# Where splits, sums, loads and searches stand in the queues of a fused attention and Fourier kernel

## The chip, the core and the metric

The kernel runs on one core of a Trainium2 chip. The engines of the core work through their own queues, each in its given order: TensorE (PE, with its weight loads shown as PEld) multiplies matrices into PSUM, VectorE (DVE) and ScalarE (ACT) do elementwise work, GpSimd (POOL) does masks and some DMAs, and SyncE (SP) issues most DMAs. An instruction waits at the head of its queue until what it needs is there, and everything behind it on that engine waits too. The metric is the device time of one execution in microseconds, as the median of several runs.

## The reference

Two independent branches share the launch; their results stand side by side in the output.

```python
def _A_ref(x, wqkv, wo):              # x (1, 2048, 1024), 32 heads of 32
    qkv = (x @ wqkv).reshape(B, S, 3, H, Dh)...
    scores = jnp.einsum("bhqd,bhkd->bhqk", q, k) * (Dh ** -0.5)
    mask = (idx[:, None] - idx[None, :] >= 0) & (idx[:, None] - idx[None, :] < 256)
    p = _softmax(jnp.where(mask, scores, -1e9), axis=-1)
    o = jnp.einsum("bhqk,bhkd->bhqd", p, v)
    return o.transpose(...).reshape(B, S, D) @ wo

def _B_ref(x, dft_seq_re, dft_seq_im, dft_hid_re, dft_hid_im):
    a = jnp.einsum("bsd,ed->bse", x, dft_hid_re)
    b = jnp.einsum("bsd,ed->bse", x, dft_hid_im)
    return jnp.einsum("ts,bse->bte", dft_seq_re, a) - jnp.einsum("ts,bse->bte", dft_seq_im, b)
```

All inputs and the output are float32. The kernel holds each float32 operand as a pair of float16 numbers, a high and a low half, and multiplies high by high, high by low and low by high.

## The kernel before

**Splitting.** `split` (line 110) makes the pair: ACT writes the high half (scaled copy, line 112), then DVE writes the low half (the scaled value minus the high half, through `vec`, line 107). Before an operand can be split its scale must be known: the largest magnitude is searched (`top` on DVE, or `u_top` on ACT with a junk output and an accumulator), PE transposes it (`pt_...`, line 145), and DVE makes the scale from it in four small instructions (`scale_of`).

**Stages.** First come 96 products for q, k and v (24 matmuls each, `product`, line 339; the list `order`). Evictions are lines 725 to 736, and the results go to scratch in DRAM. From product 24 on, the attention runs as a generator between them: every `tick` of PE work lets it go a step on (scores `s`, line 212; exponentials; a DMA transpose of the weights `hl` to `t` on SP, line 238; masks `z` and `t` on POOL, lines 250 and 252; products `pv`, line 280), until it is used up near the end.

Then comes the Fourier branch: 64 units in four rounds (two parts p by two halves c). A round has eight x units, each with two products of 24 matmuls (hidden transform, banks `p`, `un` as weights, the matrix in `reg2`; evicted on ACT, line 913), and then eight c units (sequence transform, function `seven`, line 805). A c unit does a 2 by 2 block product with seven products of 12 matmuls instead of eight, at positions 0 to 6; positions 0 to 3 and 6 are evicted by ACT (lines 809 and 824), positions 4 and 5 are added to what is there by DVE (line 811), and position 6 uses the bank of position 4 again. After position 5 and position 6 a finished 128 by 1024 result goes out, in round 0 by a plain DMA on SP, later as an accumulating store by POOL (line 952). The sums that the seven products need are made on DVE (`u_step`, line 626: raw pieces are split as `un_a`, `reg`, `un_c`, `un_b`, with four additions and subtractions, line 624, between).

Last come eight units `po` of the same seven products for the attention's output matrix wo. Its pieces are loaded, subtracted and split during the last three c units (`wo_blocks`, line 760), and the attention's output is summed in `o_blocks` (line 781, sums `r` at line 788).

**What sets the order.** The text of the kernel gives a list of things to do after each product: `do(n, turn, f, ...)` puts `f` behind position `turn` of unit n. A scheduler then lays the instructions of every engine in a queue by a timeline of its own, and may draw instructions forward or back as long as data and buffers allow. `tc.issue_after(ins)` adds an edge: what is traced in its block comes behind `ins` in the queue of their engine. `behind_act[0]` is the latest eviction that was traced on ACT, `behind[0]` the latest addition on DVE. All raw pieces of 128 by 1024 float32 (512 KB) go through a ring of six buffers, `rawp`; a load waits for the last reader of the piece six before it. The matrix of part p = 1 comes as eight pieces `wd1_...`, loaded and split into `reg2` during round 1's c units.

## Time and profile before

| | us |
|---|---|
| median of 3 runs | 1848.59 |
| runs | 1844.81 to 1850.34 |
| profiled execution, own time | 1843.89 |
| its span | 1842.1 |
| busy: PE, DVE, ACT, POOL | 1762.1, 1323.3, 1091.9, 415.7 |
| mean granted TensorE clock | 0.985 of full |

The page of the profile gives busy times, a picture of the span in 40 slices, the chain that ended last and the costliest groups. A line of the timeline reads: start in us, duration, engine, line of the kernel, instruction, what it writes and reads, sizes, count; in brackets the idle time of the engine before it and the instruction whose end released it. Buffer numbers are left out there: `p_a`, `p_b`, `p_c` are the three banks of a c unit, `raw_u` any raw piece of a unit.

In time, the q, k and v products end at about 576 us; the rounds' x units begin at about 576, 839, 1130 and 1401 us, and the `po` units at 1686.

### The profile page before, as it was taken

How to read it: one execution, taken by the hardware profiler on the slowest of the kernel's cores; microseconds unless marked ns; L12 is line 12 of the kernel's file. 1: busy time of each engine (PE TensorE's matmuls, PEld its weight loads, DVE VectorE, ACT ScalarE, POOL GpSimd, SP SyncE). 2: the span in 40 equal slices, each digit the busy share in tenths (PEclk: the TensorE clock that was granted, in tenths of full speed). 3: DMA queues.
4: the chain of work that ended last, by engine and by line, in shares of the span. 5: the costliest groups of instructions: out<-in, count | busy, mean ns of one | idle time of the engine just before them, and what ended most of it. 6: DMA issues, size and time to landing. Idle time of an engine off the chain costs nothing.

```text
span 1842.1 us, 30059 instructions
## 1 busy us (share of the span) xinstructions
PE 1762.1 (96%) x10876; PEld 857.9 (47%) x10876; DVE 1323.3 (72%) x2362; ACT 1091.9 (59%) x1867; POOL 415.7 (23%) x666
## 2 busy tenths in 40 slices
PE   7999999999999999999989899999989999888998
PEld 3444545445555545544544444545444544333443
DVE  7665787787666798776788786798776788486441
ACT  3333455465555687766777776787666787453222
POOL 0000222122213332322233234223333323100000
PEclk9999999999999999999999999999999999999999
DMA  5357899887757547778458899558999548754431
GB/s 228 122 181 204 218 236 231 220 230 171 171 127 184 117 119 182 186 180 195 101 129 187 187 200 210 104 120 185 155 163 208 118 92 140 193 108 85 122 92 69
DMA packets 440596, 297.95 MB, mean 162 GB/s; under 512 B 339072, under 2 KB 396416, under 8 KB 440448
## 3 DMA queue, kind: packets, MB, share of 16 engines
q1 hardware_dynamic: 433536, 270.87, 61.1%
q0 software_dynamic: 6912, 25.17, 8.4%
q8 instruction: 85, 1.39, 0.3%
q14 instruction: 63, 0.52, 0.1%
HBM read 146.93 MB, written 75.63 MB: 121 GB/s over the span
## 4 chain that ended last, share of the span: by engine, by line
PE 68%; DVE 10%; DMA 7%; issue 7%; ACT 6%; POOL 2%; SPq 0%; DVEq 0%; ACTq 0%; POOLq 0%
PE p L345 12%; PE p_a L817 11%; PE pk L345 9%; PE pq L345 8%; PE pv L345 8%; PE p_b L817 5%; PE po_a L817 5%; PE pv L280 3%; PE s L212 3%; DMA t<-hl 2%; PE p_c L817 2%; PE po_b L817 2%; DMA raw_wd<-in_wd_dram 2%; PE po_c L817 1%; DMA ot<-ohl 1%
## 5 line engine op out<-in xcount | busy, mean ns | idle before, releaser
L345 PE MATMUL p<-reg,un 128*128 128x512 f16 x1536 | 349.2, 379 | 5.6 <-ACT un L112 3.3
L232 ACT ACTIVATE s<-s,bias,escs 128x256 f32<-128x256 f32 (+1 forms) x512 | 269.5, 528 | 10.5
L225 ACT ACTIVATE bias<-mx,pshift,escs 128x2 f32<-128x2 f32 x256 | 98.2, 384 | 245.0 <-DVE mx L222 221.0
L236 DVE TENSOR_TENSOR hl<-s,hl 128x512 f16<-128x512 f32 (+1 forms) x256 | 170.3, 666 | 87.7 <-ACT hl L235 83.8
L345 PEld LDWEIGHTS <-un 128*128 128x128 f16 x1536 | 146.2, 98 | 169.5 <-ACT un L112 3.8
L229 POOL TENSOR_SCALAR mark<-bias 128x1 f32<-128x1 f32 x128 | 45.2, 353 | 770.7 <-ACT bias L225 770.7
L817 PE MATMUL p_a<-reg,un_c 128*128 128x512 f16 x768 | 182.6, 383 | 9.3 <-ACT y L809 5.8
L345 PE MATMUL pq<-reg,wu_q 128*128 128x512 f16 x768 | 177.5, 385 | 7.0 <-ACT reg L112 4.3
L345 PE MATMUL pk<-reg,wu_k 128*128 128x512 f16 x768 | 174.4, 379 | 0.7 <-ACT wu_k L112 0.4
L252 POOL TENSOR_SCALAR_AFFINE_SELECT t<-t 128x512 f16<-128x512 f16 x224 | 174.9, 807 | 0.1
L345 PE MATMUL pv<-reg,reg 128*128 128x512 f16 x768 | 173.6, 379 | 0.0
L222 DVE TENSOR_REDUCE mx<-s 128x2 f32<-128x512 f32 (+1 forms) x256 | 170.1, 666 | 2.5
L250 POOL TENSOR_SCALAR_AFFINE_SELECT z<-t 128x512 f16<-128x512 f16 x224 | 159.9, 735 | 51.6 <-DMA t<-hl 44.5
L235 ACT ACTIVATE hl<-s 128x512 f16<-128x512 f32 (+1 forms) x256 | 148.6, 581 | 8.7 <-DMA t<-hl 3.9
L220 DVE COPY_PREDICATED s<-upper,s 128x256 f32<-128x256 uint32 x224 | 94.3, 422 | 70.1 <-PE s L212 66.2
L212 PE MATMUL s<-qk,qk 96*128 96x128 f16 (+2 forms) x704 | 129.1, 274 | 2.3 <-DVE hl L236 1.6
L817 PEld LDWEIGHTS <-un_b 128*128 128x128 f16 x768 | 74.3, 99 | 96.6 <-issue 17.8
L345 PEld LDWEIGHTS <-wu_q 128*128 128x128 f16 x768 | 74.6, 99 | 95.5 <-issue 12.1
L280 PE MATMUL pv<-vt,t 128*128 128x65 f16 x1984 | 111.2, 186 | 8.2 <-POOL t L252 8.1
L817 PEld LDWEIGHTS <-un_c 128*128 128x128 f16 x768 | 74.5, 98 | 94.5 <-issue 11.3
L817 PEld LDWEIGHTS <-un_a 128*128 128x128 f16 x768 | 74.6, 100 | 88.7 <-issue 10.3
L345 PEld LDWEIGHTS <-reg 128*128 128x128 f16 x768 | 73.6, 98 | 83.2
(175 smaller groups left out, 2895.4 us busy)
## 6 DMA issues: line engine op xcount, KB each, us to landing
raw_u<-in_cs_dram SPq DMA_DIRECT2D x64, 512.0 KB, 4.6
qk<-qs SPq DMA_DIRECT2D x192, 128.0 KB, 3.5
out_dram<-y POOLq DMA_DIRECT2D x36, 512.0 KB, 8.0
raw_u<-in_xb_dram SPq DMA_DIRECT2D x32, 512.0 KB, 4.5
vs<-yv SPq DMA_DIRECT2D x32, 260.0 KB, 2.5
vt<-vs SPq DMA_DIRECT2D x32, 260.0 KB, 3.8
raw_x<-in_xa_dram SPq DMA_DIRECT2D x16, 512.0 KB, 10.2
qs<-yq SPq DMA_DIRECT2D x32, 256.0 KB, 2.3
```

The costliest lines, as they stand in the source:

```text
L212: nc.tensor.matmul(s[:, j, at:at + (k1 - k0) * P], q2s[g, sc][:, h, i * P:i * P + P], k2s[g, k0 // QB][:, h, k0 % QB * P:k0 % QB * P + (k1 ...
L220: nc.vector.copy_predicated(s[:, :, 2 * P:3 * P], upper2, s[:, :, :P] if nb == 3 else never2)
L222: nc.vector.tensor_reduce(mx, sv, axis=AX.X, op=ALU.max, negate=True)
L225: nc.scalar.activation(bias, mx, AF.Identity, bias=pshift, scale=es)
L232: nc.scalar.activation(sv[:, h], sv[:, h], AF.Exp, bias=bias[:, h:h + 1], scale=es)
L235: nc.scalar.activation(hi, sv, AF.Copy)
L236: behind[:] = [nc.vector.tensor_tensor(lo, sv, hi, op=ALU.subtract)]
L250: nc.gpsimd.affine_select(out=z, in_=pk, compare_op=ALU.is_gt, fill=0.0, base=0, pattern=[[0, 4], [-1, P]], channel_multiplier=1)
L252: nc.gpsimd.affine_select(out=pk, in_=pk, compare_op=ALU.is_ge, fill=0.0, base=0, pattern=[[0, 4], [1, P]], channel_multiplier=-1)
L280: nc.tensor.matmul(pvt[:, r, j, lo:], weights(part, j, kb), vts[g, k // QB][:, k % QB, at + lo:at + VW], start=(m == 0), stop=(m == len(se ...
L345: nc.tensor.matmul(ps, lhs(hl, d), rhs(hr, d), start=(m == 0), stop=(m == 3 * n - 1))
L817: nc.tensor.matmul(ps, lhs[pos](hl, k), rhs(pos)[:, hr, k], start=(m == 0 and pos < 2), stop=(m == 11), skip_group_check=True)
```

## The change

Four edits:

1. `split` takes an instruction `after`; its ACT half is then issued behind it. All splits of the units and of the `wd` pieces now pass the latest eviction.
2. In `wo_blocks` the differences (`minus`) and in `o_blocks` the two sums `r` are issued behind the latest addition on DVE.
3. Loads of c-unit pieces move from positions 5 and 6 to 1 and 3 (3 and 4 in round 1); the `wd` pieces are loaded after position 1 instead of 2 and split after position 5 instead of 3.
4. The searches of a c unit's two pieces are made in the other order, and two units ahead at positions 1 and 3 instead of 2 and 5.

```diff
-    def split(hi, lo, raw, s):
-        nc.scalar.activation(hi, raw, AF.Copy, scale=s)
+    def split(hi, lo, raw, s, after=()):
+        with tc.issue_after(after[0].ins) if after else nullcontext():
+            nc.scalar.activation(hi, raw, AF.Copy, scale=s)
...
     def wd_split():
-        piece_split(*waiting.pop(0))
+        piece_split(*waiting.pop(0), behind_act)
...
-        if j == 0:
+        if j == 1:
             tops[key] = small.tile([P, 2], F32, tag="top2", name=f"top_{key}")
...
-        if j == 1:
+        if j == 0:
             spread(key, 2)
...
-            split(u[:, 0], u[:, 1], raws.pop((n, 0)), vB[:, 1:2])
+            split(u[:, 0], u[:, 1], raws.pop((n, 0)), vB[:, 1:2], behind_act)
...
-            split(t[:, 0], t[:, 1], src, s)
+            split(t[:, 0], t[:, 1], src, s, behind_act)
...
-            split(t[:, 0], t[:, 1], r2[:, 4:], s)
+            split(t[:, 0], t[:, 1], r2[:, 4:], s, behind_act)
...
-            with tc.issue_after(behind_act[0].ins):
-                split(o[:, 0, 2 * i:2 * i + 2], o[:, 1, 2 * i:2 * i + 2], raw, vwo[:, 1:2])
-        return [lambda: (fill(0, b1), sub(b2, b2, b1)), lambda: (fill(6, b4), sub(b4, b4, b2)),
-                lambda: (fill(3, b3), sub(b1, b4, b1)), lambda: (fill(4, b2), sub(b3, b3, b4)),
+            split(o[:, 0, 2 * i:2 * i + 2], o[:, 1, 2 * i:2 * i + 2], raw, vwo[:, 1:2], behind_act)
+        def minus(o, a, b):
+            with tc.issue_after(behind[0].ins):
+                sub(o, a, b)
+        return [lambda: (fill(0, b1), minus(b2, b2, b1)), lambda: (fill(6, b4), minus(b4, b4, b2)),
+                lambda: (fill(3, b3), minus(b1, b4, b1)), lambda: (fill(4, b2), minus(b3, b3, b4)),
...
-            nc.vector.tensor_tensor(r.rearrange("p a g t -> p (a g) t"), t[:, :, 0], t[:, :, 1], op=ALU.add)
+            with tc.issue_after(behind[0].ins):
+                nc.vector.tensor_tensor(r.rearrange("p a g t -> p (a g) t"), t[:, :, 0], t[:, :, 1], op=ALU.add)
...
-                    look = (n - 2, 2), (n - 2, 5), (n - 2, 6)
+                    look = (n - 2, 1), (n - 2, 3), (n - 2, 6)
...
-                do(*look[0], u_top, n, 0)
-                do(*look[1], u_top, n, 1)
+                do(*look[0], u_top, n, 1)
+                do(*look[1], u_top, n, 0)
...
-                        do(c0 + j, 2, wd_load, 1, (j + 1) // 4, (j + 1) % 4)
-                    do(c0 + j, 3, wd_split)
+                        do(c0 + j, 1, wd_load, 1, (j + 1) // 4, (j + 1) % 4)
+                    do(c0 + j, 5, wd_split)
...
+            turns = (3, 4) if r == 1 else (1, 3)
             for j in range(3, 8):
-                do(c0 + j - 3, 5, u_load, c0 + j, 1)
-                do(c0 + j - 3, 6, u_load, c0 + j, 0)
+                do(c0 + j - 3, turns[0], u_load, c0 + j, 1)
+                do(c0 + j - 3, turns[1], u_load, c0 + j, 0)
             if r < 3:
                 for j in range(4):
-                    do(c0 + 5 + j // 2, 5 + j % 2, u_load, c0 + 8 + j)
+                    do(c0 + 5 + j // 2, turns[j % 2], u_load, c0 + 8 + j)
```

No instruction is added or removed; the queues of PE, DVE, ACT, POOL and SP are laid out anew from the middle of the v products on. Three places follow. In them the rows carry the numbers of the tiles: `un61_c` is a split operand of unit 61, `p2_60_a` bank a of c unit 60, `p1_49_0` the first product of x unit 49, `raw_wo1_0` a piece of wo, `raw_wd1_1_0` the fifth piece of the matrix of part 1.

DVE after unit 61's sums, in the wo stretch, before:

```order
L624 TENSOR_TENSOR raw_u61_0_18207<-raw_u61_0_18207,raw_u61_1_18182 128x512
L624 TENSOR_TENSOR raw_wo1_0_18509<-raw_wo1_0_18509,raw_wo0_0_18507 128x1024
L107 SCALAR_TENSOR_TENSOR un61_c_18439<-raw_u61_1_18182,sc_u61_18362,un61_c_18439 128x1024
L107 TENSOR_REDUCE top1_u62_18473<-top_u62_18424 128x1
L624 TENSOR_TENSOR raw_wo1_1_18517<-raw_wo1_1_18517,raw_wo0_1_18515 128x1024
L811 SCALAR_TENSOR_TENSOR y2_6359<-p2_60_a_18373,fu60_18205,y2_6359 128x512
L811 SCALAR_TENSOR_TENSOR y2_6359<-p2_60_b_18374,fu60_18205,y2_6359 128x512
L107 TENSOR_REDUCE sc_u62_18491<-pt_u62_18492 128x1
L107 SCALAR_TENSOR_TENSOR un61_b_18455<-raw_u61_0_18207,sc_u61_18362,un61_b_18455 128x1024
```

and with the change:

```order
L625 TENSOR_TENSOR raw_u61_0_18119<-raw_u61_0_18119,raw_u61_1_18083 128x512
L107 SCALAR_TENSOR_TENSOR un61_c_18441<-raw_u61_1_18083,sc_u61_18364,un61_c_18441 128x1024
L107 TENSOR_REDUCE top1_u62_18445<-top_u62_18409 128x1
L816 SCALAR_TENSOR_TENSOR y2_6359<-p2_60_a_18373,fu60_18207,y2_6359 128x512
L816 SCALAR_TENSOR_TENSOR y2_6359<-p2_60_b_18374,fu60_18207,y2_6359 128x512
L625 TENSOR_TENSOR raw_wo1_0_18509<-raw_wo1_0_18509,raw_wo0_0_18507 128x1024
L107 TENSOR_REDUCE sc_u62_18493<-pt_u62_18494 128x1
L107 SCALAR_TENSOR_TENSOR un61_b_18462<-raw_u61_0_18119,sc_u61_18364,un61_b_18462 128x1024
```

The first wo difference has moved behind the two additions of unit 60, the second one (`raw_wo1_1`) out of the piece, some twenty rows further down.

ACT around the split of the fifth `wd` piece, in round 1's c units, before:

```order
L809 ACTIVATE reg1_81<-p2_27_c_11690,fu27_11412 128x512
L232 ACTIVATE s_159_11615<-s_159_11615,bias_159_11629,escs_111 128x256
L235 ACTIVATE hl_159_11635<-s_159_11615 128x512
L112 ACTIVATE reg2_82<-raw_wd1_1_0_11768,vwd_102 128x1024
L809 ACTIVATE y0_6357<-p2_27_a_11688,fu27_11412 128x512
L611 ACTIVATE junk_6356,top_u29_11766<-raw_u29_0_11686 128x1024
```

and with the change:

```order
L814 ACTIVATE y2_6359<-p2_28_b_11916,fu28_11686 128x512
L113 ACTIVATE reg1_81<-raw_u29_1_11562,sc_u29_11906 128x512
L612 ACTIVATE junk_6356,top_u30_12026<-raw_u30_1_11839 128x1024
L814 ACTIVATE y1_6358<-p2_28_c_11917,fu28_11686 128x512
L113 ACTIVATE reg2_82<-raw_wd1_1_0_11751,vwd_102 128x1024
L301 ACTIVATE ohl_4_3_11966<-o_4_3_11522 128x512
```

The split has moved from unit 27 to unit 28. Its load on SP stands in both orders behind the attention's transpose `t_157`, so that two blocks of attention (`hl_158` and `hl_159`) lay between before and six (to `hl_163`) lie between now.

ACT around the split of x unit 50, before (unit 47 is a c unit of the round before):

```order
L112 ACTIVATE un49_16341<-raw_u49_0_15767,sc_B_101 128x1024
L232 ACTIVATE s_225_16042<-s_225_16042,bias_225_16064,escs_111 128x256
L235 ACTIVATE hl_224_16018<-s_224_15996 128x256
L112 ACTIVATE un50_16460<-raw_u50_0_16000,sc_B_101 128x1024
L232 ACTIVATE s_225_16042<-s_225_16042,bias_225_16064,escs_111 128x256
```

and with the change:

```order
L919 ACTIVATE y1_6358<-p1_48_1_16344,tf_103 128x512
L233 ACTIVATE s_229_16283<-s_229_16283,bias_229_16305,escs_111 128x256 x2
L236 ACTIVATE hl_229_16311<-s_229_16283 128x512
L919 ACTIVATE y2_6359<-p1_49_0_16388,tf_103 128x512
L113 ACTIVATE un50_16460<-raw_u50_0_15860,sc_B_101 128x1024
L226 ACTIVATE bias_230_16375<-mx_230_16373,pshift_93,escs_111 128x2
```

Unit 50's split has moved from the end of the round before to right behind the eviction of unit 49's first product, half a unit ahead of its use.

More of the change, by code (lines that the diff above doesn't have):

```diff
@@ L423, in wv_top, with piece_split @@
         spread(f"wv{vh}", 4)
-    def piece_split(half, i, raw, s):
-        split(reg2[:, half, 0, 2 * i:2 * i + 2], reg2[:, half, 1, 2 * i:2 * i + 2], raw, s)
+    def piece_split(half, i, raw, s, after=()):
+        split(reg2[:, half, 0, 2 * i:2 * i + 2], reg2[:, half, 1, 2 * i:2 * i + 2], raw, s, after)
     def wv_finish(vh):
```

## The prediction, on record before the run

> **What bounds the kernel now.** I read the page first, then the busy time by stretch, then every idle gap of TensorE (PE) in the timeline with what ended it, and last the other engines around the largest gaps.
>
> ```profile
> PE 1762.1 (96%) x10876; PEld 857.9 (47%) x10876; DVE 1323.3 (72%) x2362; ACT 1091.9 (59%) x1867; POOL 415.7 (23%) x666
> ```
>
> PE works through 96% of the span, so nothing but PE's own gaps (about 80 us) can be won, and each new gap is paid in full. Where they lie (columns: stretch, its length, busy us of PE, PEld, DVE, ACT, POOL, granted clock, DMA share, GB/s):
>
> ```profile
> 840.00:945.00 105.00, 99.86 (x648) 49.15 (x646) 83.62 (x142) 75.70 (x134) 29.76 (x39) 0.98 0.61 136
> 945.00:1105.00 160.00, 149.31 (x978) 73.57 (x977) 128.01 (x247) 116.47 (x203) 45.32 (x70) 0.98 0.88 182
> 1105.00:1225.00 120.00, 116.47 (x798) 58.38 (x797) 91.13 (x156) 86.14 (x151) 43.42 (x59) 1.00 0.70 149
> 1225.00:1385.00 160.00, 149.03 (x979) 74.24 (x978) 123.99 (x246) 112.02 (x201) 53.41 (x74) 0.96 0.90 164
> 1385.00:1495.00 110.00, 108.50 (x731) 53.98 (x729) 81.15 (x145) 80.07 (x143) 34.31 (x50) 0.98 0.70 139
> 1606.00:1686.00 80.00, 62.13 (x269) 26.95 (x268) 62.02 (x75) 38.17 (x46) 5.93 (x7) 0.91 0.55 119
> ```
>
> The rows are, in turn, x units and c units of round 1, the same of round 2, the x units of round 3, and the last three c units, in which the wo pieces are prepared. PE is idle 5.1, 10.7, 3.5, 11.0, 1.5 and 17.9 us. The worst stretch is the last, and VectorE (DVE) is as busy there as PE.
>
> **The wo stretch (sums behind additions).** PE's gaps and the DVE rows that end them (start, duration, instruction, in brackets the idle time before it and its releaser):
>
> ```profile
> 1609.30 0.32 PE L145 MATMUL pt_u<-ident,top_u 128*128 128x128 f32 x1 [3.03 <-DVE top_u L107]
> 1614.77 4.09 PE L817 MATMUL p_a<-reg,un_b 128*128 128x512 f16 x12 [5.15 <-DVE y L811]
> 1636.01 0.32 PE L145 MATMUL pt_u<-ident,top_u 128*128 128x128 f32 x1 [1.60 <-DVE top_u L107]
> 1636.66 2.75 PE L817 MATMUL p_a<-reg,un_b 128*128 128x512 f16 x12 [0.33 <-DVE y L811]
> 1660.79 4.97 PE L817 MATMUL p_a<-reg,un_b 128*128 128x512 f16 x12 [5.84 <-DVE y L811]
> 1670.26 0.59 PE L817 MATMUL p_a<-reg,un_c 128*128 128x512 f16 x2 [1.91 <-ACT p_c L824]
> ...
> 1606.75 1.23 DVE L624 TENSOR_TENSOR raw_wo<-raw_wo,raw_wo 128x1024 f32<-128x1024 f32 x1 [9.50 <-DMA raw_wo<-in_wo_dram]
> 1612.83 1.23 DVE L624 TENSOR_TENSOR raw_wo<-raw_wo,raw_wo 128x1024 f32<-128x1024 f32 x1 [3.59 <-DMA raw_wo<-in_wo_dram]
> 1613.97 0.74 DVE L811 SCALAR_TENSOR_TENSOR y<-p_a,fu,y 128x512 f32<-128x512 f32 x1
> 1620.66 1.29 DVE L107 SCALAR_TENSOR_TENSOR un_a<-raw_u,sc_u,un_a 128x1024 f16<-128x1024 f32 x1 [1.91 <-ACT un_a L112]
> 1629.46 1.28 DVE L107 SCALAR_TENSOR_TENSOR reg<-raw_wo,sc_wo,reg 128x1024 f16<-128x1024 f32 x1 [4.61 <-ACT reg L112]
> ```
>
> Two differences of wo pieces stand in DVE's queue ahead of unit 60's additions and wait for loads (9.50 and 3.59 us); the addition starts at 1613.97, straight after the second, and PE has by then lost 3.03 + 5.15. The gap before 1660.79 is the same addition of unit 62 behind DVE work that nobody waits for yet. The listed gaps make 17.9 us, and after the two long ones twelve products take 4.09 and 4.97 instead of 2.75: 3.6 more, so 21.5 us are lost. The change puts both additions of unit 60 ahead of every wo difference, and the second round of r sums behind unit 63's additions. How short can the stretch get? PE needs 62.1 - 3.6 = 58.5. DVE has 62.0 of work, of which the two r sums, four differences and two splits of the second block (7 us at this row's kind of duration) leave the stretch: 55, and its waits of 1.91 and 4.61 stay, because the fills hang on the same evictions as before: 61.5. Something is late next: unit 61's un_b split now stands behind the first wo difference, and the load may come 3 us later because PE's last attention block does; I allow 1.5. So 80 becomes 63: **17 us gained**. If nothing stands behind anything it is 21.5; if DVE keeps its other idle time (18 us in the row) and only the 9.5-us half of the defect goes, it is 8.
>
> **The wd pieces of round 1.** Rows of SyncE's queue (SP), ScalarE (ACT) and PE:
>
> ```profile
> 1020.18 0.44 SPq L99 DMA_DIRECT2D raw_wd<-in_wd_dram  x1
> ...
> 1026.64 1.15 ACT L112 ACTIVATE reg<-raw_wd,vwd 128x1024 f16<-128x1024 f32 x1 [5.81 <-DMA raw_wd<-in_wd_dram]
> ...
> 1028.41 5.28 PE L817 MATMUL p_a<-reg,un_c 128*128 128x512 f16 x12 [4.24 <-ACT y L809]
> 1034.30 2.75 PE L817 MATMUL p_b<-reg 128*128 128x512 f16 x12
> ```
>
> The split was queued a block or two of attention after its load; ACT stood 5.81 us, the eviction behind it came late, PE waited 4.24 and then ran at half pace (5.28 against 2.75). In the new order six blocks lie between load and split where two did, so the wait goes: 4.24 + 2.53, and some 0.6 for lesser ones: **7.4 us**. From below 0, if SP still issues the load late; from above 9.
>
> The granted clock drops after such gaps (0.91 in the wo stretch). The Trainium skill, "TensorE: Matmul & The Clock Gate", Part 1, says that PE falls to half clock after an idle window of about 3.4 us and needs as much busy time to come back; an estimate from that page is 1.7 us for each of the gaps of 4.24, 5.15 and 5.84, 5.1 together where the rows give 6.1, and the sum would be 1 us smaller. The trace disagrees on the threshold too:
>
> ```profile
> 1570.02 4.28 PE L817 MATMUL p_a<-reg,un_a 128*128 128x512 f16 x12
> ```
>
> this slow dozen follows gaps of only 2.20 and 0.94 us; the rows decide.
>
> **Loads apart from the accumulating stores.** No instruction goes; 64 loads of c units are issued two to five products earlier, while POOL's stores stay at positions 5 and 6. What they may relieve:
>
> ```profile
> 1307.22 6.64 SPq L238 DMA_TRANSPOSE t<-hl  x2
> 1313.95 8.29 SPq L303 DMA_TRANSPOSE ot<-ohl  x1
> ...
> 1318.67 0.80 POOL L250 TENSOR_SCALAR_AFFINE_SELECT z<-t 128x512 f16<-128x512 f16 x1 [6.91 <-PE s L212]
> ...
> PE pv L280 <- POOL z L250: 11.3, 6, 4.3
> PE pv L280 <- POOL t L252: 8.1, 7, 1.8
> ```
>
> Behind two loads and two stores SP takes 6 to 8 us over one or two transposes, the masks on POOL come late, and PE waits 19.4 us in all for them. The bytes are the same and a load still meets the previous unit's stores (8 us to land); between 0 and 19.4 I take **4**, nearer to nothing, since most of the crowd is the transposes themselves. The Trainium skill, "DMA: Bandwidth & Descriptors", section "Issuing engines are not separate DMA queues", says that DMAs of SP and GpSimd run interleaved on the same 16 engines; read strictly, the same bytes then take the same time and this term is 0, the sum 4 us higher.
>
> **Splits behind evictions: the x units.** Before, units 1 to 6 of a round were split two units ahead; now only after the first eviction of the unit before, 24 units in all. What covers it:
>
> ```profile
> 1190.98 0.69 ACT L913 ACTIVATE y<-p,tf 128x512 f32<-128x512 f32 x1
> ...
> 1197.07 3.19 PE L345 MATMUL p<-reg,un 128*128 128x512 f16 x14
> ...
> 1459.65 0.67 ACT L913 ACTIVATE y<-p,tf 128x512 f32<-128x512 f32 x1
> ...
> 1464.16 6.85 PE L345 MATMUL p<-reg,un 128*128 128x512 f16 x31
> ...
> 1210.22 1.04 PE L345 MATMUL p<-reg,un 128*128 128x512 f16 x4 [1.30 <-ACT un L112]
> 1212.61 6.87 PE L345 MATMUL p<-reg,un 128*128 128x512 f16 x31 [1.36 <-DVE un L107]
> ...
> L112 ACT ACTIVATE un<-raw_u,sc_B 128x1024 f16<-128x1024 f32 x32 | 36.5, 1143 | 0.4 <-PE p_a L817 0.4
> L107 DVE SCALAR_TENSOR_TENSOR un<-raw_u,sc_B,un 128x1024 f16<-128x1024 f32 x32 | 41.6, 1303 | 19.5 <-ACT un L112 19.3
> ```
>
> From the end of that eviction to the next unit's first product there are 5.4 us (1191.67 to 1197.07) and, in a tight case, 3.8 (1460.32 to 1464.16). The pair takes 1.14 + 1.30 = 2.4, so DVE may be 1.4 to 3 us late before PE notices. Unit 39 (1210.22) was split this late already and cost 1.30 + 1.36, but there another split and three copies stood between eviction and split; in the new order the split mostly stands right behind. I take 2 us for the 24; the bounds are 0 and 24 x 2.66 = 64. A round's seventh unit stays late; in rounds 0 and 3 its scale's transpose has only 2 to 3 us of PE work behind it instead of about 6, which I price at unit 39's 2.66 each, less what they lose now: **4 us lost**.
>
> **Splits and searches of the c units.** The searches come one or two products earlier in the program, yet in the new order un_c stands only 6 to 13 ACT instructions ahead of the eviction that follows its product, in ten of the fourteen later c units of rounds 0 and 2, where it stood 14 to 22 ahead; before, some c units of round 1 stood like that, with
>
> ```profile
> 968.03 0.59 PE L817 MATMUL p_a<-reg,un_c 128*128 128x512 f16 x2 [0.61 <-ACT p_c L824]
> 979.38 2.75 PE L817 MATMUL p_b<-reg 128*128 128x512 f16 x12 [0.60 <-ACT y L809]
> 1015.80 0.59 PE L817 MATMUL p_a<-reg,un_c 128*128 128x512 f16 x2 [0.41 <-ACT p_c L824]
> ```
>
> gaps of 0.4 to 0.6, a little more with what follows: 0.7 x 10 units = **7 us lost**, between 0 (attention fills) and twice that. The wd pieces of the first half move from the stretch around 400 us to 430 to 540, beside products that hardly wait: nothing; uncovered they would cost ACT's 8 x 1.15 = 9 us.
>
> **The sum.** Gains 17 + 7.4 + 4 = 28.4, losses 2 + 4 + 7 = 13: 15 us less. The profiled execution took 1843.89 us (span 1842.1 and 1.8 around it) and becomes 1828.5. It stands 4.7 under the median of the runs, so the median goes from 1848.6 to **1833**.
>
> **The rivals.** *More is won* (0.12): the crowd of transposes dissolves as well. For it: 19.4 us of PE waits hang on it; against it: the same bytes. Another 12, and the c units' 7 do not come: 1814. *DVE is the bound in the wo stretch* (0.15): its 62 us of work and its own waits stay, 8 instead of 17 are won, and with the losses 6 remain: 1842. For it: the row, where DVE equals PE; against it: half of DVE's 18 us of idle time was waits on loads. *The x units stall* (0.18), the other side: DVE, in order and 76% busy in 1105 to 1225, takes the low half late, and PE waits at each unit's third product as before 1212.61. It decides once the pair ends more than 3.8 to 5.4 us after the eviction. 24 x 1.36 = 33 in place of the 2: 1848.6 - 17 + 33 = 1864. Against it: the pair's 2.4 us. That the change does nothing is out, since hundreds of rows move on PE, DVE, ACT and SP.
>
> **Chances and range.** The forecast has 0.55, with 1820 to 1843 of its own. About 0.3% (5.5 us) is what a measurement here can tell. Faster: 0.52 of the forecast, 0.12, and 0.05 of the DVE case: 0.69. Same: 0.03 and 0.08: 0.11. Slower: 0.18 and 0.02 of the DVE case: 0.20. The range 1812 to 1860 takes in the larger win and an x-unit stall of up to 1.1 us per unit.
>
> **What would show it.** Right: no PE gap over 2 us after unit 60's additions and the last stretch near 63 us; no ACT wait on raw_wd in round 1; x units with gaps under 0.5 us. Wrong: PE waits on un at most x units; un_c or un_b as releasers in every c unit of rounds 0 and 2; a new long wait of DVE on a wo load with PE behind it.

## The result, and the profile after

The changed kernel takes 1845.27 us (median of 12 runs, 1834.52 to 1849.41); the kernel before, run beside it, takes 1845.20 (12 runs). The ratio is 0.999, with a 95% interval of 0.9971 to 1.0009: no change that these runs can tell. The forecast was 15 us less. Two executions further down, of 2305.85 and 2176.07 us, ran at a granted clock of 0.75 and 0.80; the ratios leave them out, while the medians given hold them.

The page's first part, of the changed kernel:

```profile
PE 1766.4 (96%) x10876; PEld 859.8 (47%) x10876; DVE 1321.2 (72%) x2362; ACT 1087.0 (59%) x1867; POOL 397.9 (22%) x666
```

The totals are close to those of before; by place the two kernels differ. The busy time by stretch of the changed kernel (columns as in the prediction: stretch, its length, busy us of PE, PEld, DVE, ACT, POOL, granted clock, DMA share, GB/s):

```profile
663.00:703.00 40.00, 36.84 (x206) 16.95 (x206) 31.79 (x58) 28.07 (x52) 6.41 (x8) 0.87 0.51 112
...
951.00:1115.00 164.00, 148.08 (x937) 71.64 (x935) 127.92 (x242) 117.96 (x205) 46.91 (x67) 0.96 0.89 172
...
1503.00:1539.00 36.00, 30.83 (x182) 14.56 (x181) 31.01 (x56) 25.92 (x49) 9.53 (x13) 0.91 0.44 95
...
1623.07:1685.94 62.87, 58.50 (x271) 26.31 (x269) 56.42 (x68) 37.01 (x44) 5.95 (x7) 1.00 0.72 167
```

and of the kernel before, over the same products as the last of these rows (from the last products of unit 60 to the first `po` product):

```profile
1605.90:1685.80 79.90, 62.03 (x269) 26.85 (x268) 62.02 (x75) 38.16 (x45) 5.93 (x7) 0.91 0.54 118
```

So the wo stretch shrank from 79.9 to 62.9 us, at full clock: 17.0 us won. The first and the third row of the changed kernel are new losses: the passage to the first c unit of rounds 0 and 3, with PE idle 3.2 and 5.2 us and a granted clock of 0.87 and 0.91.

To compare places that lie at other times in each kernel, I took from the trace the time from each start of a PE matmul to the next, less the usual time for a matmul of that shape, and summed it from the first product of one unit to the first of another. This lost time holds idle gaps and half pace together. By unit, in us, of the kernel before, the changed kernel and, for later, the freed kernel of the experiments:

```
units        before   changed   freed
start to 6     22.7      21.3    17.8
6 to 10         4.2      12.9     7.4
10 to 15        3.3       2.1     1.7
15 to 18        0.2       4.0     0.2
18 to 24        3.6       5.3     4.3
24 to 31       20.7      24.4     5.7
31 to 40        4.9       3.8    12.6
40 to 47       17.3      11.8     8.3
47 to 54        0.5       1.7     2.9
54 to 57        5.2      12.3     8.2
57 to 60        5.5       5.9     6.0
60 to 63       20.6       2.8     2.8
63 to end       9.1       9.3     9.3
sum           117.9     117.8    87.3
```

In the changed kernel 17.8 us are won from unit 60 to 63, and 19.6 lost from 6 to 10, 15 to 18 and 54 to 57. What ended PE's waits, over the whole span (columns: us in total, times, longest):

```profile
PE pv L281 <- POOL z L251: 17.1, 8, 4.3
PE pv L281 <- POOL t L253: 6.5, 7, 1.9
...
PE p_b L822 <- DVE top_u L107: 5.2, 3, 2.9
...
PE p_b L822 <- ACT un_b L113: 3.6, 3, 2.3
...
PE pv L281 <- DMA t<-hl: 2.1, 1, 2.1
...
PE p_a L822 <- ACT un_a L113: 1.9, 1, 1.9
...
PE p L346 <- DVE un L107: 1.0, 1, 1.0
```

Waits on `un_b`, a name that the same list of before doesn't have, are new. The first c unit of round 0 shows how they arise; ACT, then DVE, then PE of the changed kernel:

```profile
673.42 0.69 ACT L919 ACTIVATE y<-p,tf 128x512 f32<-128x512 f32 x1 [6.59 <-PE p L346]
674.00 1.14 ACT L113 ACTIVATE un_c<-raw_u,sc_u 128x1024 f16<-128x1024 f32 x1
...
678.76 0.68 ACT L919 ACTIVATE y<-p,tf 128x512 f32<-128x512 f32 x1
679.33 1.14 ACT L113 ACTIVATE un_b<-raw_u,sc_u 128x1024 f16<-128x1024 f32 x1
...
682.02 1.27 DVE L107 SCALAR_TENSOR_TENSOR un_b<-raw_u,sc_u,un_b 128x1024 f16<-128x1024 f32 x1
683.21 0.14 DVE L107 TENSOR_REDUCE top_u<-top_u 128x1 f32<-128x2 f32 x1
...
680.68 0.59 PE L822 MATMUL p_b<-reg,un_b 128*128 128x512 f16 x2
683.35 3.06 PE L822 MATMUL p_b<-reg,un_b 128*128 128x512 f16 x7 [2.07 <-DVE top_u L107]
```

and the same of the kernel before:

```profile
668.43 1.15 ACT L112 ACTIVATE un_c<-raw_u,sc_u 128x1024 f16<-128x1024 f32 x1 [0.68 <-DVE raw_u L624]
669.48 1.13 ACT L112 ACTIVATE un_b<-raw_u,sc_u 128x1024 f16<-128x1024 f32 x1
670.52 0.67 ACT L913 ACTIVATE y<-p,tf 128x512 f32<-128x512 f32 x1
...
675.55 2.11 PE L817 MATMUL p_b<-reg,un_b 128*128 128x512 f16 x9
```

Before, ACT made both splits ahead of the first eviction of x unit 7, in time that it had to spare. In the changed kernel it stands idle for 6.59 us until that eviction can run, splits `un_c` behind it and `un_b` behind the second one. PE reaches `un_b` at 680.68, its low half is finished at 683.29, and PE waits 2.07 us and then runs seven matmuls in 3.06 where nine took 2.11. The row names `top_u` as the releaser because that small reduction ended last on DVE; what PE needs is the row above it, `un_b`. Unit 56 loses the same way, 2.31 and 2.85 us at 1519.06 and 1522.52.

A second loss stands ahead of this one, at unit 8's first split, `un_a`; rows of ACT and PE of the changed kernel:

```profile
661.29 1.13 ACT L113 ACTIVATE un_a<-raw_u,sc_u 128x1024 f16<-128x1024 f32 x1
...
662.48 0.60 PE L822 MATMUL p_a<-reg,un_a 128*128 128x512 f16 x2 [1.87 <-ACT un_a L113]
663.52 1.89 PE L346 MATMUL p<-reg,un 128*128 128x512 f16 x4 [0.24 <-ACT un L113]
```

PE transposes unit 8's search result at 656.65 (653.03 before), so the scale is ready at about 661 and PE waits 1.87 us for `un_a`; four matmuls after it take 1.89 us, where the kernel before has four in 1.04.

### The profile page after: what moved, and what is told of

Its sections match the earlier page's. It is cut to its first block, busy times and chain, and to the rows that moved or that the text cites. A ratio compares the mean times of both kernels' runs of the same rounds, so it can differ in the third digit from the quotient of the medians.

```text
span 1843.2 us, 30061 instructions
## 1 busy us (share of the span) xinstructions
PE 1766.4 (96%) x10876; PEld 859.8 (47%) x10876; DVE 1321.2 (72%) x2362; ACT 1087.0 (59%) x1867; POOL 397.9 (22%) x666
## 4 chain that ended last, share of the span: by engine, by line
PE 69%; issue 11%; DVE 8%; DMA 5%; POOL 4%; ACT 2%; SPq 0%; POOLq 0%; DVEq 0%; ACTq 0%
PE p_a L822 12%; PE p L346 11%; PE pv L346 9%; PE pk L346 8%; PE pq L346 7%; PE p_b L822 6%; DMA t<-hl 5%; PE po_a L822 5%; PE pv L281 3%; PE s L213 3%; PE p_c L822 3%; PE po_b L822 2%; POOL t L253 2%; POOL z L251 2%; DVE raw_u L625 1%
## 5 line engine op out<-in xcount | busy, mean ns | idle before, releaser
L230 POOL TENSOR_SCALAR mark<-bias 128x1 f32<-128x1 f32 x128 | 49.2, 384 | 843.7 <-ACT bias L226 823.8
L822 PE MATMUL p_a<-reg,un_c 128*128 128x512 f16 x768 | 187.8, 389 | 3.7 <-ACT p_c L829 3.5
L251 POOL TENSOR_SCALAR_AFFINE_SELECT z<-t 128x512 f16<-128x512 f16 x224 | 153.3, 703 | 60.2 <-DMA t<-hl 58.2
L253 POOL TENSOR_SCALAR_AFFINE_SELECT t<-t 128x512 f16<-128x512 f16 x224 | 160.5, 741 | 0.2
L281 PE MATMUL pv<-vt,z 128*128 128x65 f16 (+1 forms) x896 | 97.8, 187 | 18.8 <-POOL z L251 17.1
## 6 DMA issues: line engine op xcount, KB each, us to landing
raw_x<-in_xa_dram SPq DMA_DIRECT2D x16, 512.0 KB, 10.2
```

Source lines behind the costliest of these rows:

```text
L251: nc.gpsimd.affine_select(out=z, in_=pk, compare_op=ALU.is_gt, fill=0.0, base=0, pattern=[[0, 4], [-1, P]], channel_multiplier=1)
L253: nc.gpsimd.affine_select(out=pk, in_=pk, compare_op=ALU.is_ge, fill=0.0, base=0, pattern=[[0, 4], [1, P]], channel_multiplier=-1)
L281: nc.tensor.matmul(pvt[:, r, j, lo:], weights(part, j, kb), vts[g, k // QB][:, k % QB, at + lo:at + VW], start=(m == 0), stop=(m == len(se ...
L822: nc.tensor.matmul(ps, lhs[pos](hl, k), rhs(pos)[:, hr, k], start=(m == 0 and pos < 2), stop=(m == 11), skip_group_check=True)
```

## The experiments

All ratios are to the kernel before, run in the same sessions. Differences between two changed kernels are of their medians, which can come from different sessions; the kernel before had medians of 1843.34 to 1846.07 us in them, so 3 us of such a difference mean little. Rows are of one execution: those of the freed kernel, of the wd part alone and of the first unit's edge alone took 1813.22, 1878.09 and 1880.38 us, 7, 14 and 15 us less than the medians, and their rows explain no more than these executions lost.

**The wo part alone.** The kernel before, with the differences and r sums behind the latest addition:

```
+        def minus(o, a, b):
+            with tc.issue_after(behind[0].ins):
+                sub(o, a, b)
...
+            with tc.issue_after(behind[0].ins):
                 nc.vector.tensor_tensor(r..., t[:, :, 0], t[:, :, 1], op=ALU.add)
```

> The kernel before with one part of the change: the wo differences, the r sums and the wo splits in their new places, nothing else. Theory T (the wo stretch wins what was forecast, and splits behind evictions around the start of a round's c units give it back): 17 to 18 us less than before, about 1828, and the profile shows TensorE's lost time from unit 60 to unit 63 fall from about 20 to about 3 us. Rival D (VectorE is the bound; time won there comes back in the output units): within 4 us of before, with new gaps after unit 63. Rival C (the DMA crowd sets the total and only moves about): within 5 us of before, with mask waits larger elsewhere.

1829.09 us against 1845.57; ratio 0.9909 (0.9879 to 0.9938): 16.5 us less. Lost time from unit 60 to 63 fell from 20.6 to 6.5, and nothing came back behind unit 63 (8.6 against 9.1). Theory T holds for this part; the rivals that the gain comes back elsewhere fall.

**The splits behind evictions, with and without the first c unit.** First all of them alone on the kernel before:

```
+        with tc.issue_after(after[0].ins) if after else nullcontext():
+            nc.scalar.activation(hi, raw, AF.Copy, scale=s)
...
-            split(u[:, 0], u[:, 1], raws.pop((n, 0)), vB[:, 1:2])
+            split(u[:, 0], u[:, 1], raws.pop((n, 0)), vB[:, 1:2], behind_act)
```

> The kernel before with one part of the change: the splits of the x units and c units behind the latest eviction. Theory T: 10 to 18 us more than before (1855 to 1863), lost at the seventh x unit, the first c unit and the second c unit's start of rounds 0 and 3 and at the start of round 1; from one x unit to the next under 0.5 us. Rival C (the crowd of DMAs carries the loss, not the splits): within 5 us of before. Rival S (the prediction's stall of every x unit): 30 us more, 1.4 at each x unit.

1879.70 us, 1.0176 (1.0141 to 1.0212): 34 us more, twice what theory T allowed. Unit 6 to 10 loses 13.8 us, the x units from 18 to 22 nothing that differs from before by 1 us. Rival S falls: the x units as such do not stall.

Then the changed kernel with the first c units free ("the freed kernel"):

```
-        s = su[n]
+        s, after = su[n], behind_act if i else ()
...
-            split(t[:, 0], t[:, 1], src, s, behind_act)
+            split(t[:, 0], t[:, 1], src, s, after)
```

> The changed kernel, with the splits of the first c unit of each round (units 8, 24, 40, 56) free of the eviction edge again, as before the change; all other edges stay. Theory T: most of the loss at units 7 to 9 (9.6 us), 55 to 57 (4.6) and some at round 1 (3.8) returns: 8 to 15 us less than the changed kernel, 1830 to 1837. Rival C: within 4 us of the changed kernel. Rival X (the x units' own splits, 7 and 55 above all, carry the loss): 0 to 4 us less.

1820.18 us, 0.9852 (0.9820 to 0.9885): 25 us less than the changed kernel. ACT's splits of unit 8 in its timeline stand ahead of the eviction again, and PE does not wait:

```profile
666.38 1.15 ACT L113 ACTIVATE un_c<-raw_u,sc_u 128x1024 f16<-128x1024 f32 x1 [3.08 <-DVE raw_u L625]
667.43 1.13 ACT L113 ACTIVATE un_b<-raw_u,sc_u 128x1024 f16<-128x1024 f32 x1
668.47 0.67 ACT L919 ACTIVATE y<-p,tf 128x512 f32<-128x512 f32 x1
...
675.55 2.11 PE L822 MATMUL p_b<-reg,un_b 128*128 128x512 f16 x9
```

The win is larger than T's 8 to 15. By the table above, 13.4 of the 30.5 us of lost time between the two profiled executions lie from 6 to 10, 15 to 18 and 54 to 57; the largest piece, 18.7, lies in round 1's c units (24 to 31), of which only the first was edited. The late `un_a` stays: PE waits 1.87 us for it here too, at 658.95, and from 6 to 10 still loses 7.4 us against 4.2 before.

> The changed kernel without the eviction edge on any split of x and c units; the wd and wo splits keep theirs. Theory T: 10 to 18 us less than the changed kernel, 1827 to 1835. Rival C: within 4 us of the changed kernel. Rival X: clearly less than the kernel that frees the first c units alone.

With no eviction edge on any of these splits: 1829.69 us, 0.9921 (0.9893 to 0.9949). That is 15.6 less than the changed kernel but 9.5 more than the freed one: in this company the edges on the other splits win something.

> The changed kernel, with only the first c units of rounds 0 and 3 (units 8 and 56) free of the eviction edge; units 24 and 40 keep it. In the profiles the freed kernel and the changed one differ by 9 us from unit 7 to 9, by 19 from unit 24 to 31 and by 4 from unit 54 to 57. If each unit's edge is paid where it stands: 9 + 4 = 13 us less than the changed kernel, 1832, and round 1 stays as it is in the changed kernel (19 us dearer than in the freed one). If the loss of round 1 is the crowd of transposes, which the first delay puts into another place, round 1 comes out different although nothing was changed there: 1818 to 1826.

```
+        s, after = su[n], () if n in (8, 56) else behind_act
```

1832.27 us, 0.9925 (0.9896 to 0.9954): 13.0 less than the changed kernel, the sum that was expected if each unit's edge is paid where it stands. But it is not paid quite there. Lost time from 6 to 10 falls by 3.9 and from 54 to 57 by 8.6; 15 to 18 and 24 to 31, where nothing was edited, fall by 3.8 and 9.9, and 31 to 40 rises by 10.3. The freed kernel, in which units 24 and 40 are free as well, loses 8.8 us less still from 24 to 31. The total agrees with the sum, the places with both theories in part.

> The changed kernel, with only the third split (un_b) of the first c unit of a round free of the eviction edge. In the changed kernel it ends 2.6, 1.7, 0.5 and 3.4 us after TensorE first needs it, while un_c has 6 to 12 us to spare. Theory: un_b alone carries the direct loss, so 10 us less than the changed kernel at least, about 1825 (1818 to 1835). Rival: within 5 us of the changed kernel, since un_b still stands behind un_c, which stays behind the first eviction.

```
+            split(t[:, 0], t[:, 1], src, s, () if i == 0 and k == "b" else behind_act)
```

1829.44 us, 0.9916 (0.9885 to 0.9946): 15.8 of the 25 us hang on the edge of `un_b` alone. From 6 to 10, 15 to 18 and 54 to 57, where the freed kernel wins 13.4 us, this one wins about 12 by the same count, and PE has no wait on `un_b` at unit 8. So most of the loss at these places hangs on `un_b`.

**The three other parts, each alone on the kernel before.**

> The kernel before with one part of the change: the loads of the c units two to five products earlier. Forecast of this part: 4 us less, 1841.5, from mask waits that fall from 19.4 us. Rival (the same bytes take the same time, so the crowd only moves): within 3 us of before, mask waits still 15 to 25. Rival (earlier loads meet the spills of attention): 5 us more.

```
+            turns = (3, 4) if r == 1 else (1, 3)
...
-                do(c0 + j - 3, 5, u_load, c0 + j, 1)
-                do(c0 + j - 3, 6, u_load, c0 + j, 0)
+                do(c0 + j - 3, turns[0], u_load, c0 + j, 1)
+                do(c0 + j - 3, turns[1], u_load, c0 + j, 0)
```

1846.76 us, 0.9998 (0.9975 to 1.0020). PE's waits on masks, of this kernel:

```profile
PE pv L280 <- POOL z L250: 13.7, 7, 4.9
PE pv L280 <- POOL t L252: 7.8, 10, 2.1
```

21.5 in all, 19.4 before. The loads relieve nothing.

> The kernel before with one part of the change: the searches of the c units one or two products earlier and in the other order. Forecast of this part by itself: no more than 3 us either way, since ScalarE is busy at two thirds and only the scale's place (unchanged at position 6) decides. Rival (a search waits for a raw piece that is not there yet and holds up the evictions behind it): 5 to 10 us more, with waits of ScalarE on raw_u.

```
-                    look = (n - 2, 2), (n - 2, 5), (n - 2, 6)
+                    look = (n - 2, 1), (n - 2, 3), (n - 2, 6)
```

1845.50 us, 1.0002 (0.9982 to 1.0022). The total is the same, its parts are not: PE's waits on POOL's masks fall to 11.1 us, while ACT's waits on wd pieces, whose splits were not touched, grow from 23.2 to 30.1 and PE waits 13.6 us for the evictions behind them (5.8 before).

> The kernel before with one part of the change: loads and splits of the wd pieces in their new places. Forecast of this part: 7.4 us less, 1838, with the wait of the split on its piece (5.81 us) and the gap of 4.24 us gone. Rival (the load is late again, or the time is lost at masks in the next units): within 3 us of before.

```
-        piece_split(*waiting.pop(0))
+        piece_split(*waiting.pop(0), behind_act)
...
-                        do(c0 + j, 2, wd_load, 1, (j + 1) // 4, (j + 1) % 4)
-                    do(c0 + j, 3, wd_split)
+                        do(c0 + j, 1, wd_load, 1, (j + 1) // 4, (j + 1) % 4)
+                    do(c0 + j, 5, wd_split)
```

1892.52 us, 1.0256 (1.0219 to 1.0294): 47 us more, which no theory had. The wait itself is gone: the view of the tile `raw_wd` has, for this kernel,

```profile
its engine sat idle before it (us, times) until:
  ACT reg L113: 7.3, 8
```

and no DMA, where the kernel before has

```profile
  DMA raw_wd<-in_wd_dram: 23.2, 12
```

The time went to the masks (33.0 us of waits against 19.4) and to one wait of 10.2 us in the wo stretch, at unit 62's transpose, behind a difference that waited 15.8 us for its load:

```profile
PE pv L281 <- POOL z L251: 25.8, 10, 6.3
PE pt_u L146 <- DVE top_u L107: 12.0, 3, 10.2
...
PE pv L281 <- POOL t L253: 7.2, 9, 1.4
```

Lost time grows most from 31 to 47 (48.2 us against 22.2), where only the last wd piece, in unit 31, is left to split. The edge also moves ACT's splits of the first half of the matrix, from 362 to 393 us to 417 to 458, and PE's order differs from 367 us on; which half costs the 47 us was not separated.

> The kernel before, with the wd loads and splits at their new turns but without the eviction edge on the splits. The queues are then those of the kernel before, except that the loads stand earlier in SyncE's. If the 47 us of the whole wd part come from the edge: within 4 us of before, and ScalarE's waits on wd pieces (23.2 us before) a little less. If they come from the turns: 30 us more or worse.

The same without `behind_act`: 1844.12 us, 0.9996 (0.9978 to 1.0014). The queues of PE, DVE and ACT are then those of before, since the scheduler draws the splits forward to their old places. The turns do nothing; the edge does everything, for better (the wait on the pieces) and worse.

**Does a part have a price of its own?** The wd edge taken out of the freed and out of the changed kernel:

```
-        piece_split(*waiting.pop(0), behind_act)
+        piece_split(*waiting.pop(0))
```

> The freed kernel (first c units without the eviction edge), with the eviction edge taken off the wd splits too; their turns stay. In the queues the attention blocks 180 to 255 then have 100 products of TensorE between a block's scores and its weighted sum, where the freed kernel has 98 (180 to 219) and 88 (220 to 255). Cover theory (the wd edge costs because it makes TensorE's order leave the masks less time): 4 to 10 us less than the freed kernel in rounds 2 and 3, against up to 7 us of ScalarE's waits on wd pieces that come back in round 1: 1812 to 1822. Rival W (the edge on the wd splits is what wins round 1): 5 to 10 us more than the freed kernel, lost at units 25 to 28, 1825 to 1830.

1854.88 us, 1.0054 (1.0028 to 1.0080): 35 us more than the freed kernel. The cover theory fails, rival W has the sign and a quarter of the size. ACT's waits on the pieces are back, and PE's behind them, with masks on top; its waits on masks and evictions, and two of ACT's rows:

```profile
PE pv L281 <- POOL z L251: 21.1, 8, 6.0
PE p_a L822 <- ACT y L814: 14.1, 4, 6.5
PE pv L281 <- POOL t L253: 8.3, 7, 3.5
...
1010.13 1.15 ACT L113 ACTIVATE reg<-raw_wd,vwd 128x1024 f16<-128x1024 f32 x1 [4.96 <-DMA raw_wd<-in_wd_dram]
1038.15 1.15 ACT L113 ACTIVATE reg<-raw_wd,vwd 128x1024 f16<-128x1024 f32 x1 [4.45 <-DMA raw_wd<-in_wd_dram]
```

> The changed kernel with the eviction edge taken off the wd splits alone. Between scores and weighted sums of blocks 180 to 219 there are then 106 products where the changed kernel has 88 (before: 108), and 102 against 86 in blocks 220 to 255 (before: 99). Cover theory: 10 to 25 us less than the changed kernel, 1820 to 1835, with mask waits down from 24 us. Rival W: 5 to 10 us more than the changed kernel.

1847.25 us, 1.0011 (0.9992 to 1.0030): 2 us more than the changed kernel, which is within the noise. Neither theory. The cover came back as counted, and mask waits went to 27.4 us all the same. So the distance in products between scores and weighted sum does not set them alone.

> The kernel before, with one edge alone: the splits of the first c unit of each round (8, 24, 40, 56) behind the latest eviction. If this edge costs by itself what it cost in the changed kernel: 15 to 25 us more than before, 1860 to 1870, with TensorE's waits on un_b and top_u at units 8 and 56. If only the mixture of all edges makes it dear: within 6 us of before.

```
+        s, after = su[n], () if i else behind_act
```

(the kernel before, with this edge as its only change) 1895.22 us, 1.0267 (1.0243 to 1.0292): 49 us more. Waits on `un_b` at units 8, 40 and 56 are there (1.6, 1.0 and 2.8 us), yet they are the small part:

```profile
PE pv L281 <- POOL z L251: 22.7, 13, 4.5
PE p_a L818 <- DVE y L812: 12.1, 8, 4.2
PE p_a L818 <- ACT y L810: 11.0, 5, 3.8
PE pv L281 <- DMA t<-hl: 10.3, 2, 5.8
...
PE pv L281 <- POOL t L253: 4.3, 8, 1.0
```

37.3 us of mask waits instead of 19.4, and 11.0 behind ACT's evictions instead of 5.8.

> The kernel before with the splits of x and c units behind the latest eviction, but for the first c units of the rounds. All splits with these cost 34 us. If the first units' edge carries the loss: 15 to 34 us less than that, 1845 to 1863; if the remaining edges win by themselves the 9.5 us by which the freed kernel beats the one without any edge on splits: 1836. If the loss is in the order as a whole: still 1870 or more.

1868.74 us, 1.0112 (1.0083 to 1.0141): 21 us more than before by the ratio, and 11 or 12 less than with the first units. The first unit's edge costs that much here, 25 in the changed kernel and 49 alone.

> The freed kernel with the loads of the c units at their old turns. The queues of TensorE, VectorE and ScalarE are the same in both, only SyncE's differ. If the loads are worth nothing, as alone on the kernel before (0.9998): within 4 us of the freed kernel, 1816 to 1824. Forecast of this part: 4 us more. If they matter once ScalarE's splits stand elsewhere (the raw ring of six): 5 to 15 us more.

1818.82 us, 0.9853 (0.9827 to 0.9879), within 1.4 us of the freed kernel: for the second time the loads are worth nothing.

> The freed kernel with the searches of the c units at their old places. The order of all engines then differs from the freed kernel's in most units. If a search's place matters little: within 6 us of the freed kernel, 1814 to 1826. If any shift of the order is worth tens of us through the masks: outside of that, on either side, and TensorE's waits on masks differ by as much.

1844.83 us, 0.9997 (0.9973 to 1.0021): 25 us more than the freed kernel, mask waits 35.0 against 15.5. Alone, the searches were worth nothing.

> The changed kernel with the searches at their old places. Searches alone on the kernel before: no difference; taken out of the freed kernel: 25 us more. If a search's place has a price of its own: 0 or 25 us more than the changed kernel, as in one of the two. If it counts through the order of the queues alone, it can also be less than the changed kernel; TensorE's waits on masks (24 us in the changed kernel) then go the same way.

1856.61 us, 1.0064 (1.0045 to 1.0084): 11 us more than the changed kernel, mask waits 38.1 against 25.7. Searches at their new places are worth 0, 11 or 25 us, by company.

> The freed kernel with the wo part at its old places. Up to unit 60 its queues are those of the freed kernel. If a part that moves no queue ahead of it adds up: 17 us more than the freed kernel, 1837 (the wo part alone on the kernel before won 16.5). If nothing adds up in this kernel: less than 5 or more than 30.

1834.68 us, 0.9955 (0.9936 to 0.9975): 14.5 us more than the freed kernel by the medians, 19 by the ratios, 17 expected. The part that leaves the queues ahead of it as they are has about the same price in both kernels (16.5, and 14.5 to 19).

**Mask waits side by side** (PE's waits of `pv` on `z`, `t` and the transposes, in us, from the view of waits of one execution each; the four kernels of the first line have the same queues on PE, DVE and ACT, and so have the three of the second, up to unit 60 where they differ by the wo part; each of the others has an order of its own):

```
before 19.4, wo alone 18.7, loads alone 21.5, wd turns alone 20.1
freed 15.5, freed without loads 13.3, freed without wo 15.9
searches alone 11.8   changed 25.7   no split edges 18.2
wd part alone 33.0    first unit's edge alone 37.3
freed without searches 35.0   changed without searches 38.1
changed with 8 and 56 free 18.6   with un_b free 23.4   without wd edge 27.4
freed without wd edge 30.0   splits without first units 31.1   splits alone 36.7
```

Within each of the first two lines they agree to 3 us; over all orders they go from 12 to 38. They belong to the order of the queues, and an edge at one unit gives another order, hundreds of rows long, for the rest of the program.

## Why the prediction was wrong

**The wo stretch: right, to the microsecond.** "So 80 becomes 63": 79.9 became 62.9, with PE at 58.5 busy as forecast and DVE at 56.4 (forecast 55). The part alone won 16.5 us and cost 14.5 to 19 when it was taken out of the freed kernel. That the time agrees to a tenth is in part luck: what is late next is not unit 61's `un_b`, for which the forecast allowed 1.5 us, but unit 61's additions, which stand behind two wo splits on DVE (PE waits 1.77 us at 1644.58).

**The wd pieces: the wait went, the gain didn't stay.** ACT's 23.2 us of waits on the pieces are gone, with the gap of 4.24 at PE. Yet 24 to 31 still loses 24.4 us (20.7 before), with mask waits where the wd wait was. PE's waits in that stretch, of the changed kernel (951 to 1118 us):

```profile
PE pv L281 <- POOL z L251: 8.9, 4, 4.3
PE pv L281 <- POOL t L253: 1.9, 1, 1.9
```

and of the kernel before (939 to 1104 us):

```profile
PE p_a L817 <- ACT y L809: 4.2, 1, 4.2
PE pv L280 <- POOL z L250: 2.9, 2, 2.4
...
PE pv L280 <- POOL t L252: 1.4, 1, 1.4
```

The freed kernel has 0.2 us of mask waits there. The edge is worth 35 us in the freed kernel, nothing that can be told in the changed one, and costs 47 alone. The term of 7.4 priced the one wait and took the rest of the queue as given.

**Loads apart: 4 forecast, 0 measured,** twice with equal queues. (The prediction speaks of 64 loads of c units; the edit moves five c units of eight in a round, 40 loads, and 12 loads of x units, by two to four products.) The rule of the Trainium skill that the prediction weighed, "DMA: Bandwidth & Descriptors", section "Issuing engines are not separate DMA queues", gave 0 when read strictly; these two runs agree with it (0.9998 alone; 1818.82 against 1820.18).

**Splits behind evictions: the step that failed.** The prediction watched the 24 x units (2 us, bound 64) and the later c units of rounds 0 and 2 (7 us). The x units do not stall: PE waits 1.2 us on `un` in the changed kernel, 5.5 before. The c units from 10 to 15 and 40 to 47 lose 6.7 us less than before. The step that failed is the one on the passage from x units to c units: "in rounds 0 and 3 its scale's transpose has only 2 to 3 us of PE work behind it instead of about 6 ... **4 us lost**". The scale is late at unit 8 much as forecast: PE waits 1.87 us for `un_a`, and this stays in the freed kernel. What the term put at nothing is the first c unit's third split, `un_b`. Its place in the text is behind the second product of x unit 7; the scheduler had drawn it forward into ACT's idle time (669.48 before), and the edge forbids that (679.33 after). From 6 to 10, 15 to 18 and 54 to 57 the changed kernel loses 19.6 us more than before, 13.4 of which go when the first c units are freed; in the whole kernel freeing them brings 25, and 15.8 of that with `un_b` alone. I priced the edge by the instructions that it was put behind, not by what the scheduler had been doing for that split.

**The sum of terms.** The forecast added parts. That the total came out at nothing, inside the range of 1812 to 1860, is a coincidence of places: 17.8 us won from 60 to 63 and 6.7 in c units of rounds 0 and 2, 19.6 lost at the passages and 3.7 in round 1's c units. Two of the three signs of being right came true (the wo stretch, no ACT wait on `raw_wd`) and the third but for one wait of 1.0 us on `un`; none of them looked at the passages. Only the wo part and the loads, at 0, add up; the wd edge, the searches and the first units' edge range over tens of us with the company they are in, since each reorders the queues behind it and mask waits go from 12 to 38 us with the order. That term, of unknown sign, was missing, and the 7.4, 4, 2, 4 and 7 were all smaller than it. With 20.7 and 17.3 us of lost time in round 1's and 2's c units, the sum should have carried a term of that size, either way.

**What stays open.** Which property of an order makes masks late. Distance between scores and weighted sum is not it by itself. Mask waits are also not the whole: with searches alone they fell by 7.6 us, and the waits on wd pieces took it back. Of the 18.7 us by which round 1's c units differ between the changed and the freed kernel, 9.9 go with the edges of units 8 and 56 and 8.8 with those of 24 and 40, but each step also moves time to other units (31 to 40 rises by 10.3 in the first), so no edge has a price there that can be read off.

**A version that beats both.** The freed kernel, at 0.9852, is 25 us under either; without the moved loads it is the same (0.9853).

## What to carry to other kernels

Where a scheduler draws work forward into idle time, an edge that pins it behind another instruction takes that freedom from every use of the helper; look for the one use whose text stands latest (here the first unit after a change of loop) and leave it free. A part that sits at the end of the program, or leaves the queues ahead of it and behind it as they are, can be priced from the profile (17 forecast, 14.5 to 19 measured); a part that reorders queues must be measured in the company it will have, and its price alone says little. If the sum of good terms comes out at nothing, take the parts out of the whole one by one, not only alone.

## What the runs showed of the hardware

PE ran at half pace after short gaps here too: 2.07 us idle at 683.35, then seven matmuls in 3.06 us (nine take 2.11). The granted clock of 0.87 over the 40 us around it holds two such stretches, the other one behind the wait of 1.87 us for `un_a` (columns as above):

```profile
662.00:671.00 9.00, 7.44 (x42) 3.11 (x43) 8.67 (x16) 4.79 (x10) 4.19 (x4) 0.62 0.97 193
...
683.00:688.00 5.00, 4.66 (x15) 1.97 (x16) 4.63 (x13) 3.41 (x8) 0.00 (x0) 0.66 0.66 157
```

The prediction had noted the same after 2.20 and 0.94 us. The length of a single gap doesn't decide: twelve matmuls take 4.44 us, where 2.75 is full pace, behind gaps of 0.84 and 0.91 us close together:

```profile
832.11 0.61 PE L822 MATMUL p_b<-reg,un_b 128*128 128x512 f16 x2 [0.84 <-ACT un_b L113]
833.62 4.44 PE L822 MATMUL p_a<-reg,un_c 128*128 128x512 f16 x12 [0.91 <-ACT p_c L829]
```

In the wo stretch, where no gap exceeds 1.77 us after the change, the granted clock is 1.00:

```profile
1644.58 2.75 PE L822 MATMUL p_a<-reg,un_b 128*128 128x512 f16 x12 [1.77 <-DVE y L816]
```

the twelve products behind that gap take 2.75 us, full pace.
